# Key cache of a decode step: the second and third pair of heads loaded in one transfer of 64 KB rows

## Chip, cores and metric

The kernel runs on one core of a Trainium2 chip. The metric is the device time of one execution in microseconds (us), lower is better. Several executions were timed, and one was recorded by the hardware profiler; "span" is the time from the first to the last instruction of that execution.

## What is computed

One decode step for one token of width 512: attention over a cache of 16384 keys and values with 8 key/value heads of 128 and 32 query heads (four to a key/value head), then a small block whose sequence mixer sees a sequence of length one, and an MLP.

```python
h  = x + A(layernorm(x))                # A: attention over the cache
h2 = h + B(layernorm(h))                # B: mixer + MLP, weights w1..w4

# A, for the 8 key/value heads:
q = (x @ wq).reshape(1, 1, 32, 128)     # 32 query heads
scores = q @ k^T * 128 ** -0.5          # k_cache [1, 8, 16384, 128], bf16
p = softmax(scores)
o = p @ v                               # v_cache [1, 8, 16384, 128], bf16
A = o.reshape(1, 1, 4096) @ wo

# B: with a sequence of one, every shifted quarter of the mixer is padding (zero),
# so x1 = x, and what is left is
B = x + gelu(layernorm(x) @ w3) @ w4
```

The keys and values together are 67 MB of the 79 MB that are read.

## The kernel before

The heads are worked on in four **pairs** (`PAIRS = 4`). For one pair the keys are 8 MB, laid out over 128 partitions with one row of 64 KB in each (`pair_rows`: 64 partitions for each of the two heads, 256 keys in each partition). The values lie the same way in `vb`. There is one key buffer `kb_all` of 64 KB a partition, cut into two halves `kb[0]` and `kb[1]`, and one value buffer `vb`.

Key loads: pair 0 comes in one load of 8 MB. Pairs 1 to 3 come in two loads of 4 MB (`load_keys(j, y)`), one for each half `y`, and each is issued when the transposes of that half of the pair before have been read out. Value loads: one of 8 MB a pair (`load_values`), issued when the value matmuls of the pair before are done; POOL waits for it with a nop, which releases TensorE. All of these go through SP's queue, in the order of the program: wq, keys 0, values 0, keys 1 (two halves), values 1, and so on; after the keys of pair 3 and the values of pair 3 the weights `wo` (two loads), `w3` and `w4` (four loads), which reuse `kb`.

For one pair the work runs as follows:

1. VectorE transposes the keys (`transpose_keys`, L616) from `kb` into `kt`, half by half; `kt` holds one half. A half has eight pieces; an instruction does one or two of them (`cuts`). A piece was made of two runs of 2 KB, one in each half of the row's half.
2. TensorE computes the scores (`scores`): a clearing matmul (L627) for each half and four matmuls for each of its eight pieces (L633), in a loop with registers, which waits on VectorE's semaphore before every piece.
3. `softmax`: maximum (`mx`, L643), its exchange between partitions over TensorE (L647), exponentials on ScalarE (L655), two transposes into `pt` (L659).
4. Meanwhile TensorE runs a loop of matmuls whose result nobody reads (`P.spin`, fourteen passes of two, L498). Behind that loop, in TensorE's order, come the sum of the softmax (`sums`, L678) and the value matmuls (`values`, L670).
5. `gather` (L687 to L696) brings the result together, and the next pair begins.

TensorE's program for a pair is one loop body that is run four times (`_tensor`). The waits and offsets that change from piece to piece and from pair to pair are held in registers. After the last pair come the product with `wo` (L739), the layer norm, the products with `w3` (L759) and `w4` (L782, L794) and the output.

Of the kernel before, what the change touches and what calls it, by code (L numbers as in the profile page):

```python
# [7 lines left out]
BF16 = mybir.dt.bfloat16  # L8
I32 = mybir.dt.int32
# [340 lines left out]
DH = 128  # L350
# [11 lines left out]
PAIRS = HKV // 2  # L362
RPARTS = 9
QPAD = 4 * 7
KP = 8 * DH
QW = QPAD + 128
SCALE = 1.0 / math.sqrt(DH)
EPS = 1e-5
# [2 lines left out]
def bass_sequential_preLN__gqa_block_cached__mixer_s_mlp__decode_kernel(  # L371
# [13 lines left out]
    with ExitStack() as ctx:  # L385
        sb = lambda name, shape, dt: ctx.enter_context(nc.sbuf_tensor(name, shape, dt))
        ps = lambda name, shape, dt: ctx.enter_context(nc.psum_tensor(name, shape, dt))
        P = Program(nc, ctx)
# [54 lines left out]
        hT = sb("hT", [128, NCH, 32], FP32)  # L443
        hcol = sb("hcol", [128, NHC, 32], BF16)
        fin = sb("fin", [64, 256], BF16)
        kb_all = sb("kb", [128, 256 * DH], BF16)
        kb = [kb_all[:, i * 128 * DH:(i + 1) * 128 * DH] for i in range(2)]
        vb = sb("vb", [128, 256 * DH], BF16)
        kt = sb("kt", [128, 128 * DH], BF16)
# [12 lines left out]
        def load(name, dst, src, key, by="SP", also=()):  # L462
            P.op(by, lambda e: e.dma_start(dst, src), w=[key, *also], dma=name)

        def pair_rows(src, j):
            return src[0, 2 * j:2 * j + 2].rearrange("g (u t) d -> (g u) (t d)", u=64)

        def load_keys(j, y):
            n = 128 * DH
            load(f"k{y}", kb[y][:, :], pair_rows(A_k_cache, j)[:, y * n:(y + 1) * n], ("r", y, 0),  # L470
                 also=[("r", y, i) for i in range(1, RPARTS)])

        def load_values(j):
            load("v", vb[:, :], pair_rows(A_v_cache, j), ("v", 0), also=[("landed", 0)])
# [19 lines left out]
        def copies(col, n):  # L494
# [4 lines left out]
                                      start=True, stop=True)  # L499
# [27 lines left out]
        def variance(i):  # L527
# [7 lines left out]
            for n in range(1 + i):  # L535
# [6 lines left out]

        load("x4", x4[:, :], A_x[0, 0:1, :].rearrange("o (q j) -> (o q) j", q=4), "x4", "ACT")
        load("wq", wq_sb[:, 0:NCH * HQ * DH], A_wq.rearrange("(p k) c -> p (k c)", k=NCH), ("v", 0), also=[("v", x) for x in range(1, VP)])
        load("k", kb_all[:, :], pair_rows(A_k_cache, 0), ("r", 0, 0),
             also=[("r", y, i) for y in range(2) for i in range(RPARTS) if y or i])

        dve(lambda e: e.memset(mean4[:, :], -1.0 / (32 * D)), w=["mean4"])
        dve(lambda e: e.memset(ident_f[:, :], 0.0), w=["ident_f"])
# [8 lines left out]
            r=["ident", "x4"], w=["quarter"])  # L558
        pe(lambda e: e.matmul(O_ps[0][:, 0:128], quarter[:, :, :].rearrange("p q u -> p (q u)"), x4[:, :],
                              start=True, stop=True), r=["quarter"], w=[("O", 0)], bank=[("O", 0)])  # L560
# [7 lines left out]
             r=["ident_f"], w=["swapped"])  # L568

        dve(lambda e: e.tensor_reduce(row32[:, :], ident_f[:, :].rearrange("p (c r) -> p r c", c=4), AX.X, ALU.add),  # L570
            r=["ident_f"], w=["row32"])
        dve(lambda e: e.tensor_reduce(maskdd[:, :], ident_f[:, :].rearrange("p (n d) -> p d n", d=4), AX.X, ALU.add),
            r=["ident_f"], w=["maskdd"])
# [35 lines left out]
                qcol[lo:hi, :, :, 0].rearrange("p n (j h) -> p n j h", h=REP)), r=["qcol"], w=["qb"])  # L609


        def transpose_keys(y, cuts):
            for t, n in zip(cuts, [b - a for a, b in zip(cuts, [*cuts[1:], 8])]):
                view = lambda x, t=t, n=n: x[:, :].bitcast(I32).rearrange("p (x l w) -> p x (l w)", x=2, l=64)[
                    :, :, t * 512:(t + n) * 512]
                P.op("DVE", lambda e, view=view: e.transpose(view(kt), view(kb[y])),  # L616
                     r=[("r", y, i) for i in range(RPARTS)], w=[("kt", t + i) for i in range(n)], worth=n)

        def key_piece(at, n):
            part = kt[:, :].rearrange("p (x f) -> p x f", x=2)[:, :, bass.ds(at, KP)]  # L620
            return part.rearrange("p x (l b s e) -> p b e x l s", l=8, b=2, s=32, e=2)[:, n // 2, n % 2, :, :, :]

        none = qn[:, 0, 0:1]

# [35 lines left out]
                    r=["p"], w=["pt"])  # L660

        def values(j):
            tiles = vb[:, :].rearrange("p (x c l d) -> p x l c d", x=4, c=8, l=8)
            for x in range(VP):
                P.part("value", j, x)
                for it in range(16 // VP):
                    for ct in range(4):
                        l, ch = 2 * it + ct // 2, ct % 2
                        l += 32 // VP * x
                        pe(lambda e, l=l, ct=ct, ch=ch: e.matmul(  # L670
                            O_ps[0][32 * ct:32 * ct + 32, :], pt[:, l, ch, :, :].rearrange("p g u -> p (g u)"),
                            tiles[:, l // 8, l % 8, 4 * ch:4 * ch + 4, :], start=(l < 2), stop=(l >= 30)),
                           r=[("landed", x), "pt"], w=[("O", 0)], bank=[("O", 0)])

        def sums(j):

            P.spin(14)
            pe(lambda e: e.matmul(n_ps[0:32, 32:33], zd[:, :], acc[:, :], start=True, stop=True),  # L678
               r=["acc", "zd", "pt"], w=["n"], bank=["mn"])
            dve(lambda e: e.reciprocal(den[:, :], n_ps[0:32, 32:33]), r=["n"], w=["den"], bank=["mn"])  # L680
# [21 lines left out]
        for j in range(PAIRS):  # L702
            P.part("query", j)
            dve(lambda e, j=j: e.tensor_copy(qn[:, :, :], qb[:, :, j, :]), r=["qb"], w=["qn"])
            for y in range(2):
                P.part("half", j, y)
                transpose_keys(y, (0, 2, 4, 6) if j < PAIRS - 1 else range(8) if y else (0, 1, 2, 4, 6))
                scores(j, y)
                if j < PAIRS - 1:
                    load_keys(j + 1, y)  # L710
            P.part("middle", j)
            softmax(j)
            sums(j)
            values(j)
            P.part("rest", j)
            gather(j)
            if j < PAIRS - 1:
                load_values(j + 1)
# [29 lines left out]
        s = st[1]  # L748
# [87 lines left out]
```

## Time and profile before

| | |
|---|---|
| median of 3 executions | 189.88 us (189.8 to 190.06) |
| the profiled execution | 189.89 us, span 188.4 us |
| VectorE, TensorE matmuls, ScalarE, busy | 115.8, 137.8, 9.3 us |
| DMA | 79.19 MB, 2605 packets, mean 420 GB/s over the span |
| SP's queue, share of the 16 engines | 97.9% |
| keys, values | 2 x 4 MB a pair (pair 0: 8 MB), 8 MB a pair |

How to read the rows that follow: the profile lists instructions by source line (L616 is line 616 of the kernel before), engine and operation. DVE is VectorE, PE the matmuls of TensorE, PEld its weight loads, ACT ScalarE, POOL GpSimd, SPq the instruction stream of SyncE, which issues the loads. A row of a timeline begins with the start in us from the span's start and the length in us; x8 counts merged instructions; the square bracket is the idle time of that engine just before, and what ended it. Rows of the list of DMA issues end with the us from issue to landing. Where no bracket stands, the engine had no idle time to speak of.

### The profile page before, as it was taken

To read this page: it belongs to the slowest core of one execution; us is meant where nothing else is said; L and a number is where in the kernel's file an instruction comes from. 1 tells how busy PE (TensorE), PEld (TensorE's weight loads), DVE (VectorE), ACT (ScalarE), POOL (GpSimd) and SP (SyncE) were. 2 spreads that over 40 slices of the span, in tenths; PEclk is the share of its full clock that TensorE was granted. 3 is DMA by queue.
4 is the path that set the end of the run, shared out by engine and by line. 5 is a ranking of instruction groups with operands and counts; after the bars stand their busy time and mean duration, and the time that the engine had idled before them with its cause. 6 is when DMAs were issued, how large, how long until landed. Compare 5 with 4: busy or idle time off the path is not lost.

```text
span 188.4 us, 2532 instructions
## 1 busy us (share of the span) xinstructions
PE 137.8 (73%) x820; PEld 59.3 (31%) x824; DVE 115.8 (61%) x141; ACT 9.3 (5%) x16; POOL 5.9 (3%) x11
## 2 busy tenths in 40 slices
PE   1009700599989639998990999999319999886874
PEld 1004200234434413443450344345103433432332
DVE  4900741999645299994508999551449897513154
ACT  3000000000020000000200000020000000500011
POOL 1900000000000000000000000000000000000010
PEclk9999985569999975999998599999955999999998
DMA  6999999999799998999999999997999998899994
GB/s 223 445 445 445 445 445 445 445 445 445 334 445 445 445 543 362 417 389 403 445 445 445 445 445 445 445 445 334 445 445 445 556 403 362 362 440 450 397 411 183
DMA packets 2605, 79.19 MB, mean 420 GB/s; under 512 B 298, under 2 KB 300, under 8 KB 812
## 3 DMA queue, kind: packets, MB, share of 16 engines
q1 hardware_dynamic: 2596, 79.17, 97.9%
q8 instruction: 1, 0.02, 0.0%
q10 hardware_dynamic: 8, 0.00, 0.0%
HBM read 79.17 MB, written 0.00 MB: 420 GB/s over the span
## 4 chain that ended last, share of the span: by engine, by line
DMA 45%; PE 36%; DVE 16%; issue 2%; ACT 0%; SPq 0%; DVEq 0%
DMA kb<-in_A_k_cache_dram 32%; PE banks L633 22%; DMA kb<-in_B_w_dram 13%; DVE kt L616 12%; PE banks L498 6%; PE banks L670 4%; DVE mx L643 1%; PE banks L627 1%; DVE od L690 1%; PE banks L647 1%; PE banks L759 1%; PE banks L694 0%; DVE od L687 0%; DVE osum L785 0%; PE banks L782 0%
## 5 line engine op out<-in xcount | busy, mean ns | idle before, releaser
L616 DVE STREAM_TRANSPOSE kt<-kb 128x2048 int32<-128x2048 int32 (+1 forms) x37 | 71.0, 1985 | 10.4 <-DMA kb<-in_A_k_cache_dram 10.4
L633 PE MATMUL banks<-kt,qn 128*128 x256 | 69.1, 426 | 0.1
L633 PEld LDWEIGHTS banks<-kt,qn 128*128 x256 | 26.8, 105 | 41.0 <-issue 21.5
L498 PE MATMUL banks<-xn 128*128 128x512 bf16 x126 | 28.6, 381 | 0.0
L627 PE MATMUL banks<-qn 128*128 128x512 bf16 x8 | 3.9, 490 | 23.9 <-DVE kt L616 23.9
L498 PEld LDWEIGHTS banks<-xn 128*128 128x128 bf16 x130 | 12.7, 99 | 15.8 <-issue 2.4
L593 PE MATMUL banks<-vb,xn 128*128 x32 | 8.5, 432 | 9.7 <-DVE xn L584 9.7
L670 PE MATMUL banks<-vb,pt 128*32 128x512 bf16 x256 | 14.7, 379 | 0.7 <-POOLq L475 0.7
L659 DVE STREAM_TRANSPOSE pt<-p_sb 64x1024 bf16<-64x1024 bf16 x8 | 9.9, 1239 | 5.4 <-ACT p_sb L655 5.3
L655 ACT ACTIVATE p_sb<-banks,bias 128x1024 bf16<-128x1024 f32 x4 | 4.5, 1114 | 155.4 <-DVE nmh L651 155.4
L670 PEld LDWEIGHTS banks<-vb,pt 128*32 128x32 bf16 x256 | 8.7, 97 | 4.7 <-POOLq L475 0.8
L687 DVE TENSOR_SCALAR od<-banks,rowc 128x128 f32<-128x128 f32 x4 | 1.4, 351 | 14.2 <-PE banks L670 14.2
L643 DVE TENSOR_REDUCE mx<-banks 128x1 f32<-128x1024 f32 x4 | 4.9, 1224 | 8.1 <-PE banks L633 8.1
L627 PEld LDWEIGHTS banks<-qn 128*128 128x128 bf16 x8 | 0.8, 100 | 25.8 <-issue 25.4
L600 DVE STREAM_TRANSPOSE qcol<-banks 64x1024 f32<-64x1024 f32 x4 | 4.8, 1226 | 6.6 <-PE banks L593 6.6
L593 PEld LDWEIGHTS banks<-vb,xn 128*128 128x128 bf16 x32 | 3.5, 108 | 14.3 <-issue 11.6
L539 POOL TENSOR_TENSOR st<-st,expo 128x1 f32<-128x1 f32 (+1 forms) x2 | 1.3, 630 | 175.4 <-DVE st L537 175.4
L506 PE MATMUL banks<-mean 128*128 128x512 f32 (+1 forms) x12 | 6.5, 622 | 0.0
L694 PE MATMUL banks<-od,zo 128*32 128x128 f32 x8 | 1.6, 285 | 6.5 <-DVE od L690 6.5
L680 DVE RECIPROCAL den<-banks 32x1 f32<-32x1 f32 x4 | 0.6, 155 | 7.8 <-PE banks L678 7.8
L690 DVE SCALAR_TENSOR_TENSOR od<-banks,rowc,od 128x128 f32<-128x128 f32 x12 | 4.2, 351 | 0.4
L647 PE MATMUL banks<-mxd,mean 128*128 128x128 f32 x8 | 2.0, 326 | 2.4 <-DVE mxd L644 2.4
(81 smaller groups left out, 49.5 us busy)
## 6 DMA issues: line engine op xcount, KB each, us to landing
kb<-in_A_k_cache_dram SPq DMA_DIRECT2D x6, 4096.0 KB, 24.9
vb<-in_A_wq_dram SPq DMA_DIRECT2D x1, 4096.0 KB, 12.3
kb<-in_A_wo_dram SPq DMA_DIRECT2D x1, 3584.0 KB, 28.5
kb<-in_B_w_dram SPq DMA_DIRECT2D x1, 1792.0 KB, 24.2
kb<-in_B_w_dram SPq DMA_DIRECT2D x1, 896.0 KB, 26.0
kb<-in_B_w_dram SPq DMA_DIRECT2D x1, 640.0 KB, 27.1
kb<-in_A_wo_dram SPq DMA_DIRECT2D x1, 512.0 KB, 29.4
kb<-in_B_w_dram SPq DMA_DIRECT2D x1, 256.0 KB, 27.2
```

What stands on the lines that cost most here:

```text
L498: P.unread = lambda e: e.matmul(banks[:, 7, :], copies(xn[:, 0:1], 128), copies(xn[:, 0:1], 512), start=True, stop=True)
L506: pe(lambda e: e.matmul(banks[:, 7, 0:n], mean4[:, :], copies(mean4[:, 0:1], n), start=True, stop=True), r=["mean4"], w=["spare1"])
L593: pe(lambda e, k=k: e.matmul(row[:, bass.ds(P.b, 512)], copies(xn[:, k:k + 1], 128), wq_k[:, k, bass.ds(P.c, REP * DH)], start=(k == 0), s ...
L600: dve(lambda e, g=g, b=b, half=half: e.transpose(qcol[64 * g:64 * g + 64, 2 * b:2 * b + 2, :, :].rearrange("p e m u -> p (e m u)"), half.r ...
L616: P.op("DVE", lambda e, view=view: e.transpose(view(kt), view(kb[y])), r=[("r", y, i) for i in range(RPARTS)], w=[("kt", t + i) for i in r ...
L627: pe(lambda e: e.matmul(row[:, bass.ds(P.y, 512)], copies(none, 128), copies(none, 512), start=True, stop=False, skip_group_check=True), r ...
L633: pe(lambda e, n=n: e.matmul(row[:, bass.ds(P.y, 512)], qn[:, n, bass.ds(P.q, 128)], key_piece(P.k, n), start=False, stop=(n == 3), skip_g ...
L643: dve(lambda e: e.tensor_reduce(mx[:, :], s_all, AX.X, ALU.max), r=[("s", 0), ("s", 1)], w=["mx"], **both)
L655: act(lambda e: e.activation(p_sb[:, :], s_all, ACTF.Exp, bias=bias[:, 0:1], scale=float(SCALE), accum_out=acc[:, :]), r=[("s", 0), ("s", ...
L659: dve(lambda e, g=g: e.transpose(pt[64 * g:64 * g + 64, :, :, g, :], p_sb[64 * g:64 * g + 64, :]), r=["p"], w=["pt"])
L670: pe(lambda e, l=l, ct=ct, ch=ch: e.matmul(O_ps[0][32 * ct:32 * ct + 32, :], pt[:, l, ch, :, :].rearrange("p g u -> p (g u)"), tiles[:, l ...
L690: dve(lambda e, block=block, c=c: e.scalar_tensor_tensor(od[:, :], block, rowc[:, c:c + 1], od[:, :], ALU.mult, ALU.add), r=[key, "rowc", ...
```

## The change

The keys of pairs 1 and 2 come in one load of 8 MB (64 KB a row), as those of pair 0 do; pair 3 keeps its two halves. To let such a load begin before the pair ahead has been read to the end, the key buffer grows by 8 KB a partition and each pair's keys lie 4 KB lower than those of the pair before (`BASE`): pair 0 at 8 KB, pair 1 at 4 KB, pairs 2 and 3 at 0. The last sixteenth of pair 0 and of pair 1 thus lies above what the next load writes; the instruction that reads it has a key of its own (`tail`), and the load waits for the other fifteen sixteenths alone. For this the last two pieces of the second half are transposed one by one.

A piece is now one contiguous sixteenth of the row (4 KB) in place of two runs of 2 KB, with the views of `key_piece` and `values` to match; `KP`, the step of a piece, doubles. The loop of unread matmuls runs eleven passes in place of fourteen in every pair. The first half of pair 3 is transposed in four instructions of two pieces, where it was two of one and three of two.

```diff
--- before.py
+++ after.py
@@ -362,7 +362,8 @@
 PAIRS = HKV // 2
 RPARTS = 9
 QPAD = 4 * 7
-KP = 8 * DH
+KP = 16 * DH
+BASE = (2 * KP, KP, 0, 0)
 QW = QPAD + 128
 SCALE = 1.0 / math.sqrt(DH)
 EPS = 1e-5
@@ -443,7 +444,7 @@
         hT = sb("hT", [128, NCH, 32], FP32)
         hcol = sb("hcol", [128, NHC, 32], BF16)
         fin = sb("fin", [64, 256], BF16)
-        kb_all = sb("kb", [128, 256 * DH], BF16)
+        kb_all = sb("kb", [128, BASE[0] + 256 * DH], BF16)
         kb = [kb_all[:, i * 128 * DH:(i + 1) * 128 * DH] for i in range(2)]
         vb = sb("vb", [128, 256 * DH], BF16)
         kt = sb("kt", [128, 128 * DH], BF16)
@@ -465,10 +466,14 @@
         def pair_rows(src, j):
             return src[0, 2 * j:2 * j + 2].rearrange("g (u t) d -> (g u) (t d)", u=64)
 
-        def load_keys(j, y):
+        def load_keys(j, y=None):
             n = 128 * DH
-            load(f"k{y}", kb[y][:, :], pair_rows(A_k_cache, j)[:, y * n:(y + 1) * n], ("r", y, 0),
-                 also=[("r", y, i) for i in range(1, RPARTS)])
+            if y is None:
+                load("k", kb_all[:, BASE[j]:BASE[j] + 2 * n], pair_rows(A_k_cache, j), ("r", 0, 0),
+                     also=[("r", y, i) for y in range(2) for i in range(RPARTS) if y or i] + [("tail", j)])
+            else:
+                load(f"k{y}", kb[y][:, :], pair_rows(A_k_cache, j)[:, y * n:(y + 1) * n], ("r", y, 0),
+                     also=[("r", y, i) for i in range(1, RPARTS)])
 
         def load_values(j):
             load("v", vb[:, :], pair_rows(A_v_cache, j), ("v", 0), also=[("landed", 0)])
@@ -542,8 +547,7 @@
 
         load("x4", x4[:, :], A_x[0, 0:1, :].rearrange("o (q j) -> (o q) j", q=4), "x4", "ACT")
         load("wq", wq_sb[:, 0:NCH * HQ * DH], A_wq.rearrange("(p k) c -> p (k c)", k=NCH), ("v", 0), also=[("v", x) for x in range(1, VP)])
-        load("k", kb_all[:, :], pair_rows(A_k_cache, 0), ("r", 0, 0),
-             also=[("r", y, i) for y in range(2) for i in range(RPARTS) if y or i])
+        load_keys(0)
 
         dve(lambda e: e.memset(mean4[:, :], -1.0 / (32 * D)), w=["mean4"])
         dve(lambda e: e.memset(ident_f[:, :], 0.0), w=["ident_f"])
@@ -609,16 +613,18 @@
                 qcol[lo:hi, :, :, 0].rearrange("p n (j h) -> p n j h", h=REP)), r=["qcol"], w=["qb"])
 
 
-        def transpose_keys(y, cuts):
+        def transpose_keys(j, y, cuts):
             for t, n in zip(cuts, [b - a for a, b in zip(cuts, [*cuts[1:], 8])]):
-                view = lambda x, t=t, n=n: x[:, :].bitcast(I32).rearrange("p (x l w) -> p x (l w)", x=2, l=64)[
-                    :, :, t * 512:(t + n) * 512]
-                P.op("DVE", lambda e, view=view: e.transpose(view(kt), view(kb[y])),
-                     r=[("r", y, i) for i in range(RPARTS)], w=[("kt", t + i) for i in range(n)], worth=n)
+                at = BASE[j] + (8 * y + t) * KP
+                apart = BASE[j] and y and t == 7
+                P.op("DVE", lambda e, t=t, n=n, at=at: e.transpose(
+                    kt[:, t * KP:(t + n) * KP].bitcast(I32), kb_all[:, at:at + n * KP].bitcast(I32)),
+                     r=[("tail", j)] if apart else [("r", y, i) for i in range(RPARTS)],
+                     w=[("kt", t + i) for i in range(n)], worth=n)
 
         def key_piece(at, n):
-            part = kt[:, :].rearrange("p (x f) -> p x f", x=2)[:, :, bass.ds(at, KP)]
-            return part.rearrange("p x (l b s e) -> p b e x l s", l=8, b=2, s=32, e=2)[:, n // 2, n % 2, :, :, :]
+            part = kt[:, bass.ds(at, KP)]
+            return part.rearrange("p (l b s e) -> p b e l s", l=16, b=2, s=32, e=2)[:, n // 2, n % 2, :, :]
 
         none = qn[:, 0, 0:1]
 
@@ -660,7 +666,7 @@
                     r=["p"], w=["pt"])
 
         def values(j):
-            tiles = vb[:, :].rearrange("p (x c l d) -> p x l c d", x=4, c=8, l=8)
+            tiles = vb[:, :].rearrange("p (y c x l d) -> p y x l c d", y=2, c=8, x=2, l=8)
             for x in range(VP):
                 P.part("value", j, x)
                 for it in range(16 // VP):
@@ -669,12 +675,12 @@
                         l += 32 // VP * x
                         pe(lambda e, l=l, ct=ct, ch=ch: e.matmul(
                             O_ps[0][32 * ct:32 * ct + 32, :], pt[:, l, ch, :, :].rearrange("p g u -> p (g u)"),
-                            tiles[:, l // 8, l % 8, 4 * ch:4 * ch + 4, :], start=(l < 2), stop=(l >= 30)),
+                            tiles[:, l // 16, l // 8 % 2, l % 8, 4 * ch:4 * ch + 4, :], start=(l < 2), stop=(l >= 30)),
                            r=[("landed", x), "pt"], w=[("O", 0)], bank=[("O", 0)])
 
         def sums(j):
 
-            P.spin(14)
+            P.spin(11)
             pe(lambda e: e.matmul(n_ps[0:32, 32:33], zd[:, :], acc[:, :], start=True, stop=True),
                r=["acc", "zd", "pt"], w=["n"], bank=["mn"])
             dve(lambda e: e.reciprocal(den[:, :], n_ps[0:32, 32:33]), r=["n"], w=["den"], bank=["mn"])
@@ -704,10 +710,12 @@
             dve(lambda e, j=j: e.tensor_copy(qn[:, :, :], qb[:, :, j, :]), r=["qb"], w=["qn"])
             for y in range(2):
                 P.part("half", j, y)
-                transpose_keys(y, (0, 2, 4, 6) if j < PAIRS - 1 else range(8) if y else (0, 1, 2, 4, 6))
+                transpose_keys(j, y, range(8) if y and j == PAIRS - 1 else (0, 2, 4, 6, 7) if y else (0, 2, 4, 6))
                 scores(j, y)
-                if j < PAIRS - 1:
+                if j == PAIRS - 2:
                     load_keys(j + 1, y)
+                elif j < PAIRS - 2 and y:
+                    load_keys(j + 1)
             P.part("middle", j)
             softmax(j)
             sums(j)
```

## The prediction

> **What bounds the kernel now.** I read the page first: the share of the DMA engines and the chain of waits.
>
> ```profile
> span 188.4 us, 2532 instructions
> q1 hardware_dynamic: 2596, 79.17, 97.9%
> DMA 45%; PE 36%; DVE 16%; issue 2%; ACT 0%; SPq 0%; DVEq 0%
> ```
>
> The one load queue is busy for 97.9% of the span, and the chain changes hands between transfers and computing. So I laid the queue's own timetable (the timeline of SP: start and length of each issue) beside the landings (the list of DMA issues, asked for around one issue at a time; the last number is us from issue to landing).
>
> ```profile
> 0.74 0.40 SPq L463 DMA_DIRECT2D vb<-in_A_wq_dram  x1
> 1.19 0.42 SPq L463 DMA_DIRECT2D kb<-in_A_k_cache_dram  x1
> 22.43 0.33 SPq L463 DMA_DIRECT2D vb<-in_A_v_cache_dram  x1
> 50.16 0.33 SPq L463 DMA_DIRECT2D kb<-in_A_k_cache_dram  x1
> 64.38 0.33 SPq L463 DMA_DIRECT2D vb<-in_A_v_cache_dram  x1
> 133.21 0.33 SPq L463 DMA_DIRECT2D vb<-in_A_v_cache_dram  x1
> ```
> ```profile
> vb<-in_A_wq_dram SPq DMA_DIRECT2D x1, 4096.0 KB, 12.3
> kb<-in_A_k_cache_dram SPq DMA_DIRECT2D x1, 31.2
> vb<-in_A_v_cache_dram SPq DMA_DIRECT2D x1, 29.3
> kb<-in_A_k_cache_dram SPq DMA_DIRECT2D x1, 4096.0 KB, 21.0
> vb<-in_A_v_cache_dram SPq DMA_DIRECT2D x1, 26.1
> vb<-in_A_v_cache_dram SPq DMA_DIRECT2D x1, 34.9
> ```
>
> Issue plus time to landing: wq at 13.0, first keys at 32.4, first values at 51.7, the second half of pair 1's keys at 71.2, pair 1's values at 90.5, pair 3's values at 168.1. Steps: an 8 MB load takes 19.3 us, two 4 MB loads 71.2 - 51.7 = 19.5, the next 8 MB 19.3. The queue runs without a hole, and a pair costs it 38.8 us.
>
> Then the VectorE timeline, where each pair's work begins and ends.
>
> ```profile
> 32.47 17.66 DVE L616 STREAM_TRANSPOSE kt<-kb 128x2048 int32<-128x2048 int32 x8 [6.46 <-DMA kb<-in_A_k_cache_dram]
> 52.43 1.22 DVE L643 TENSOR_REDUCE mx<-banks 128x1 f32<-128x1024 f32 x1 [2.29 <-PE banks L633]
> 66.84 17.64 DVE L616 STREAM_TRANSPOSE kt<-kb 128x2048 int32<-128x2048 int32 x8
> 86.77 1.23 DVE L643 TENSOR_REDUCE mx<-banks 128x1 f32<-128x1024 f32 x1 [2.29 <-PE banks L633]
> 101.30 17.66 DVE L616 STREAM_TRANSPOSE kt<-kb 128x2048 int32<-128x2048 int32 x8
> 121.25 1.22 DVE L643 TENSOR_REDUCE mx<-banks 128x1 f32<-128x1024 f32 x1 [2.29 <-PE banks L633]
> 139.04 8.95 DVE L616 STREAM_TRANSPOSE kt<-kb 128x1024 int32<-128x1024 int32 x5 [3.17 <-DMA kb<-in_A_k_cache_dram]
> 148.74 9.13 DVE L616 STREAM_TRANSPOSE kt<-kb 128x1024 int32<-128x1024 int32 x8 [0.75 <-DMA kb<-in_A_k_cache_dram]
> 159.12 1.22 DVE L643 TENSOR_REDUCE mx<-banks 128x1 f32<-128x1024 f32 x1 [1.25 <-PE banks L633]
> ```
>
> Pairs 1 and 2 have no idle time before their first transpose: keys were there, and VectorE and TensorE set the pace, 34.4 us a pair (101.30 - 66.84). That is 4.4 us a pair less than the queue needs, so computing, late after the start, has caught up with the queue at pair 3: it waits 3.17 us for the first half of the keys. From there transfers lead, but by little.
>
> ```profile
> 60.58 0.40 PE L670 MATMUL banks<-vb,pt 128*32 128x512 bf16 x3
> 161.04 6.29 PE L498 MATMUL banks<-xn 128*128 128x512 bf16 x28
> 163.08 2.49 DVE L659 STREAM_TRANSPOSE pt<-p_sb 64x1024 bf16<-64x1024 bf16 x2 [1.33 <-ACT p_sb L655]
> 168.16 0.40 PE L670 MATMUL banks<-vb,pt 128*32 128x512 bf16 x4 [0.67 <-POOLq L475]
> 176.71 1.91 PE L739 MATMUL banks<-kb,o_b 128*32 128x512 bf16 x32 [0.17 <-DMA kb<-in_A_wo_dram]
> 182.29 0.94 PE L759 MATMUL banks<-kb,hc 128*32 128x448 bf16 x16 [0.34 <-DMA kb<-in_B_w_dram]
> 186.60 0.12 PEld L794 LDWEIGHTS banks<-kb,hcol 128*32 128x32 bf16 x8 [0.20 <-DMA kb<-in_B_w_dram]
> ```
>
> The value matmuls of pair 3, and each of the three weight products behind them, wait for their load by 0.67, 0.17, 0.34 and 0.20 us (POOL's nop stands for the values' landing). That is all the cover a later computing chain has.
>
> **The change part by part.**
>
> *One load in place of two, for pairs 1 and 2.* The queue gains the difference of 19.5 and 19.3 or 19.4, about 0.1 us a pair by landings rounded to 0.1; bounds 0 and 0.2 each. I take 0.1 twice.
>
> The Trainium skill (DMA: Bandwidth & Descriptors, "Anatomy of one DMA") fits a load's time, for the path of GpSimd, as 2.0 us plus its bytes over 436 GB/s. If those 2 us occupied the queue, two loads fewer would give 4 us; the steps above show some 0.1, because the next load streams meanwhile.
>
> *The issue moves from the half to fifteen sixteenths.* Before, pair 1's first half was issued when half of pair 0 was transposed. Now SP waits for seven instructions of two pieces and one of one piece: 17.66 less one piece, 9.13 / 8 = 1.14, so 16.5, with one more start 16.6, and the issue stands at 32.47 + 16.6 = 49.1. The queue drains at 51.7. What an issue needs before its bytes flow is seen at the start: wq lands 12.3 us after its issue, of which 4 MB are 19.3 / 2 = 9.7, so 2.6. 49.1 + 2.6 = 51.7: exactly in time. Below, no gain is possible, since bytes cannot flow before the queue is empty; above, the wq figure is from an empty queue and the same lead recurs at pair 2, so I allow 0 to 0.6 us a load and take 0. Pair 1's keys then land at 71.1, its values at 90.4, pair 2's keys at 109.8. Behind SP's longer wait stand only later loads. The value load of pair 1 goes out at 64.38 less what the loop saves, 63.1, and is needed by 71.1 - 2.6 = 68.5. With the steps below and the 3.8 us from value matmuls to issue (64.38 - 60.58), those of pairs 2 and 3 go out 30.6 us after a pair's first transpose, at 101.8 and 140.5, and are needed by 107.2 and 145.9: 5 us of cover each.
>
> *No transpose before 8 MB have landed.* This is the cost. Pair 2 began at 101.30; now it begins at 109.9. From first transpose to `mx` the three full pairs take 19.96, 19.93 and 19.95 us, so `mx` stands at 129.85.
>
> *The last two pieces of a pair in two instructions.* They come one by one, so one might take the 2.29 us before `mx` for 1.25, as pair 3 has it. The weight loads of pair 1's last three pieces speak against that:
>
> ```profile
> 83.57 0.66 PEld L633 LDWEIGHTS banks<-kt,qn 128*128 x4 [0.22 <-issue]
> 84.64 0.56 PEld L633 LDWEIGHTS banks<-kt,qn 128*128 x4 [0.41 <-issue]
> 85.69 0.56 PEld L633 LDWEIGHTS banks<-kt,qn 128*128 x4 [0.49 <-issue]
> ```
>
> They follow each other every 1.05 us with idle time put to "issue": TensorE's sequencer needs that long for a turn of its loop, whichever piece lies ready. Bounds: 0 and 1.04 us; I take 0.
>
> *Eleven passes in place of fourteen.* 28 matmuls take 6.29 us, so six fewer take 6 x 0.22 = 1.3 off. This counts whole: `pt` is ready at 163.08 + 2.49 = 165.57, before even the shortened loop ends at 161.04 + 6.29 - 1.3 = 166.0.
>
> *Contiguous pieces, other strides for scores and values.* The same elements in the same number of matmuls; I take 0, bounds minus and plus 0.1 us a pair (the four transposing stretches above differ by 0.02).
>
> *The sum.* From `mx` to the next pair's first transpose: 66.84 - 52.43 = 14.4 and 101.30 - 86.77 = 14.5; less 1.3 it is 13.2. Pair 3 begins at 129.85 + 13.2 = 143.05 in place of 139.04; both halves of its keys are there by then or before they are needed (138.9 and 148.5, against 143.05 and 151.9). Its `mx` stands at 143.05 + 19.95 = 163.0 in place of 159.12. From `mx` to the value matmuls pair 0, which had its values, took 60.58 - 52.43 = 8.15; less 1.3 it is 6.85, so 169.85 in place of 168.16: 1.7 us later, and now behind its load (167.9), not waiting for it. The later waits fall away one after another: 1.7 - 0.17 - 0.34 - 0.20 = 1.0. The profiled execution took 189.89 us with a span of 188.4; 1.0 on it gives **190.9**. Its time is that of the median (189.88), so no correction between the two.
>
> One cost has a range of its own: TensorE's clock at the beginning of a pair.
>
> ```profile
> 34.92 0.61 PE L627 MATMUL banks<-qn 128*128 128x512 bf16 x1 [12.60 <-DVE kt L616]
> 39.00:41.00 2.00, 2.00 (x7) 0.59 0.68 295
> 41.00:43.00 2.00, 2.00 (x11) 1.00 1.21 524
> ```
>
> The windows' column after the count is the granted clock: half until about 40.6 (0.59 of that stretch), so 5.7 us after the first matmul. Pairs 2 and 3 will start at other moments and may find other such stretches.
>
> The Trainium skill (TensorE: Matmul & The Clock Gate, Part 1) says that activity is judged in free-running windows of 3.4 us, so that a cold stretch lies between one and two windows, up to 6.8 us. By that rule a bad phase is 1.1 us colder than here, half of which is lost work: up to 0.5 us a pair, and the sum would be 191.9; none of it in a good phase, since the sequencer and the transposes hold the pace then. Trace and rule agree as far as 5.7 lies between; I take 0 and keep it for the range.
>
> **The rivals.**
>
> *The last piece alone shortens the score tail.* If the loop turn hides nothing, pair 2 gives back 1.04 us; pair 3 has its eight single pieces already. Then 1.7 becomes 0.7, which the same waits swallow, and what is left is the queue's 0.2: 189.7. For it: pair 3's 1.25. Against it: the three weight-load rows.
>
> *The issue comes too late.* Each miss opens a hole in the queue that moves everything after it, computing included. With 0.6 us at both loads 190.9 + 1.2 = 192.1. For it: the lead of 2.6 is no longer than the start-up of 2.6. Against it: the engines need not be idle when the new load's descriptors arrive, and part of the 2.6 is landing, not starting.
>
> *Faster: long rows stream better than the landings show.* If the merged load saved more than 0.5 us each time, pair 2's keys would land over 1.0 us earlier, everything behind would move along, and the loss above be gone; at 1.0 us each the time is 190.9 - 1.8 = 189.1. The steps of 19.3 to 19.5 us leave hardly room for it: the 64 KB rows are in the trace already, as first keys and values.
>
> **How the numbers follow.** My forecast 0.70 (its own range 190.5 to 191.9, with the clock's phase and the strides); short tail 0.13, no change; late issue 0.14, slower; better streaming 0.03, faster. What a measurement of this kernel can tell from no change is about 0.2%, 0.4 us. The range of eight in ten leaves out the fast side, most of the short tail and the worst of the late issues: 190.0 to 192.4. Faster 0.03, same 0.13, slower 0.84.
>
> **What would show it.** Right: SP's second key issue near 49.1 with no hole at 51.7; pair 2's first transpose near 109.9, pair 3's near 143 without an idle time for DMA; value matmuls of pair 3 near 169.9 with no wait for POOL; the waits before the three weight products gone. Wrong: 1.3 instead of 2.3 us before `mx` in pairs 0 to 2 (short tail); key loads landing later than 71.1 and 109.8 (late issue) or clearly earlier (streaming). If pair 3 still idles for its keys, my chain through pair 2 is too long.

## The result, and the profile after

| | before | changed |
|---|---|---|
| median of 6 executions | 189.75 us (189.62 to 190.06) | 190.67 us (190.45 to 190.97) |
| the profiled execution | 189.89 us, span 188.4 us | 190.69 us, span 189.4 us |

The changed kernel is slower: ratio 1.0048, 95% interval 1.0037 to 1.0058. The forecast was 190.9. (Lines have moved: L616 is now L620, L627 L633, L633 L639, L643 L649, L670 L676, L739 L747, L759 L767, L794 L802.)

The page first.

```profile
span 189.4 us, 2456 instructions
q1 hardware_dynamic: 2308, 79.17, 97.3%
DMA 40%; PE 37%; DVE 19%; issue 3%; ACT 0%; SPq 0%; DVEq 0%
```

The same bytes in 288 packets fewer; in the chain that ended last, 5% of the span has gone from DMA, three of the five to VectorE. SP's timeline and the landings (us from issue to landing, asked for around each issue) say where.

```profile
22.96 0.33 SPq L464 DMA_DIRECT2D vb<-in_A_v_cache_dram  x1
49.26 0.33 SPq L464 DMA_DIRECT2D kb<-in_A_k_cache_dram  x1
63.17 0.33 SPq L464 DMA_DIRECT2D vb<-in_A_v_cache_dram  x1
87.97 0.33 SPq L464 DMA_DIRECT2D kb<-in_A_k_cache_dram  x1
101.87 0.33 SPq L464 DMA_DIRECT2D vb<-in_A_v_cache_dram  x1
140.57 0.33 SPq L464 DMA_DIRECT2D vb<-in_A_v_cache_dram  x1
```
```profile
vb<-in_A_v_cache_dram SPq DMA_DIRECT2D x1, 28.9
kb<-in_A_k_cache_dram SPq DMA_DIRECT2D x1, 21.9
vb<-in_A_v_cache_dram SPq DMA_DIRECT2D x1, 27.4
kb<-in_A_k_cache_dram SPq DMA_DIRECT2D x1, 21.9
vb<-in_A_v_cache_dram SPq DMA_DIRECT2D x1, 27.5
```

The first values, issued at 22.96, land at 51.9; pair 1's keys at 71.2, its values at 90.6, pair 2's keys at 109.9, pair 3's values at 168.1. Each 8 MB still takes 19.3 us, so the queue has no hole (no time without bytes) in this execution. The lead, the time from a key load's issue until the load ahead of it has landed, was only 2.6 us both times (51.9 - 49.26, 90.6 - 87.97). The whole stream ends where it did; what has moved is the computing:

```profile
71.30 17.72 DVE L620 STREAM_TRANSPOSE kt<-kb 128x2048 int32<-128x2048 int32 x9 [5.61 <-DMA kb<-in_A_k_cache_dram]
91.23 1.22 DVE L649 TENSOR_REDUCE mx<-banks 128x1 f32<-128x1024 f32 x1 [2.21 <-PE banks L639]
110.00 17.72 DVE L620 STREAM_TRANSPOSE kt<-kb 128x2048 int32<-128x2048 int32 x9 [5.47 <-DMA kb<-in_A_k_cache_dram]
129.93 1.23 DVE L649 TENSOR_REDUCE mx<-banks 128x1 f32<-128x1024 f32 x1 [2.21 <-PE banks L639]
143.14 17.90 DVE L620 STREAM_TRANSPOSE kt<-kb 128x2048 int32<-128x2048 int32 x12
163.07 1.23 DVE L649 TENSOR_REDUCE mx<-banks 128x1 f32<-128x1024 f32 x1 [2.03 <-PE banks L639]
```

VectorE, which never waited for the keys of pairs 1 and 2, now waits 5.61 and 5.47 us for their 8 MB. Pair 3, which waited 3.17 us for its keys, no longer waits at all (no bracket) and begins 4.1 us later than before. TensorE, from there to the end:

```profile
165.00 4.97 PE L503 MATMUL banks<-xn 128*128 128x512 bf16 x22
169.91 0.40 PE L676 MATMUL banks<-vb,pt 128*32 128x512 bf16 x3
178.29 1.91 PE L747 MATMUL banks<-kb,o_b 128*32 128x512 bf16 x32
183.46 0.94 PE L767 MATMUL banks<-kb,hc 128*32 128x448 bf16 x16
187.26 0.57 PE L802 MATMUL banks<-kb,hcol 128*32 128x128 bf16 x28
```

The brackets that named a load at the value matmuls and at the three weight products are gone. The lateness shrinks along these rows: 169.91 - 168.16 = 1.75 us at the value matmuls, 1.58 at L747, 1.17 at L767. The end of the span is 1.0 later.

### The profile page after: what moved, and what is told of

The parts are those of the page before. It is cut to its first block, busy times and chain, and to the rows that moved or that the text cites. A ratio compares the mean times of both kernels' runs of the same rounds, so it can differ in the third digit from the quotient of the medians.

```text
span 189.4 us, 2456 instructions
## 1 busy us (share of the span) xinstructions
PE 131.4 (69%) x796; PEld 57.0 (30%) x800; DVE 115.9 (61%) x143; ACT 9.3 (5%) x16; POOL 5.9 (3%) x11
## 4 chain that ended last, share of the span: by engine, by line
DMA 40%; PE 37%; DVE 19%; issue 3%; ACT 0%; SPq 0%; DVEq 0%
DMA kb<-in_A_k_cache_dram 40%; PE banks L639 22%; DVE kt L620 14%; PE banks L503 7%; PE banks L676 4%; DVE mx L649 1%; PE banks L633 1%; DVE od L696 1%; PE banks L747 1%; PE banks L653 1%; PE banks L511 1%; PE banks L767 0%; PE banks L700 0%; DVE od L693 0%; DVE osum L793 0%
## 5 line engine op out<-in xcount | busy, mean ns | idle before, releaser
L620 DVE STREAM_TRANSPOSE kt<-kb 128x2048 int32<-128x2048 int32 (+1 forms) x39 | 71.1, 1891 | 17.1 <-DMA kb<-in_A_k_cache_dram 17.1
L639 PE MATMUL banks<-kt,qn 128*128 x256 | 67.7, 416 | 0.0
L639 PEld LDWEIGHTS banks<-kt,qn 128*128 x256 | 26.4, 103 | 40.0 <-issue 20.8
L633 PE MATMUL banks<-qn 128*128 128x512 bf16 x8 | 3.9, 492 | 32.6 <-DVE kt L620 32.6
L503 PE MATMUL banks<-xn 128*128 128x512 bf16 x102 | 23.3, 381 | 0.0
L676 PE MATMUL banks<-vb,pt 128*32 128x512 bf16 x256 | 14.8, 379 | 0.0
L503 PEld LDWEIGHTS banks<-xn 128*128 128x128 bf16 x106 | 10.3, 99 | 12.9 <-issue 2.4
L633 PEld LDWEIGHTS banks<-qn 128*128 128x128 bf16 x8 | 0.8, 100 | 34.7 <-issue 34.4
L676 PEld LDWEIGHTS banks<-vb,pt 128*32 128x32 bf16 x256 | 9.5, 97 | 3.3
L649 DVE TENSOR_REDUCE mx<-banks 128x1 f32<-128x1024 f32 x4 | 4.9, 1224 | 8.7 <-PE banks L639 8.7
L585 DVE COPY zo<-rowgh 128x32 f32<-128x32 f32 x1 | 3.6, 3628 | 0.0
L585 DVE COPY zd<-maskgh 128x32 f32<-128x32 f32 x1 | 3.6, 3557 | 0.0
## 6 DMA issues: line engine op xcount, KB each, us to landing
kb<-in_A_k_cache_dram SPq DMA_DIRECT2D x2, 4096.0 KB, 20.5
```

Source lines behind the costliest of these rows:

```text
L503: P.unread = lambda e: e.matmul(banks[:, 7, :], copies(xn[:, 0:1], 128), copies(xn[:, 0:1], 512), start=True, stop=True)
L585: dve(lambda e, z=z, m=m: e.tensor_copy(z[:, :].rearrange("p (n d) -> p n d", d=4), m[:, :, :].rearrange("p g h -> p (g h)").unsqueeze(2). ...
L620: P.op("DVE", lambda e, t=t, n=n, at=at: e.transpose(kt[:, t * KP:(t + n) * KP].bitcast(I32), kb_all[:, at:at + n * KP].bitcast(I32)), r=[ ...
L633: pe(lambda e: e.matmul(row[:, bass.ds(P.y, 512)], copies(none, 128), copies(none, 512), start=True, stop=False, skip_group_check=True), r ...
L639: pe(lambda e, n=n: e.matmul(row[:, bass.ds(P.y, 512)], qn[:, n, bass.ds(P.q, 128)], key_piece(P.k, n), start=False, stop=(n == 3), skip_g ...
L649: dve(lambda e: e.tensor_reduce(mx[:, :], s_all, AX.X, ALU.max), r=[("s", 0), ("s", 1)], w=["mx"], **both)
```

## The experiments

All were run beside the kernel before, in three series, each on one chip: p1_only, p2_only, spin14 and before_spin11 (the kernel before: 189.81); shift2_spin14, no_shift, spin9 and p1_lead (189.86); after_again, shift2, shift2_spin9 and p1_shift4 (189.91). The record doesn't name the chip of the first result above.

**Which pair costs: p1_only and p2_only.** The edits to the changed kernel:

```diff
# p1_only                                   # p2_only
-BASE = (2 * KP, KP, 0, 0)
+BASE = (KP, 0, 0, 0)                       # BASE = (KP, KP, 0, 0)
-if j == PAIRS - 2:
-    load_keys(j + 1, y)
-elif j < PAIRS - 2 and y:
-    load_keys(j + 1)
+if 1 <= j <= PAIRS - 2:                    # if j in (0, PAIRS - 2):
+    load_keys(j + 1, y)
+elif j == 0 and y:                         # elif j < PAIRS - 2 and y:
+    load_keys(j + 1)
```

In p2_only the halves of pair 1 are also placed at `BASE[j]`, and the key of its own (`apart`) holds for pair 1 alone.

> Only pair 1's keys come in one load; pair 2's come in two halves again (buffers shifted once, by 4 KB). Theory (cover): the loss is made at pair 2, whose transposes start only when 8 MB have landed and whose lateness reaches the end through pair 3; pair 1's late start is absorbed. So pair 2 starts at 71.3 + 33.1 = 104.4 as soon as pair 1 is done, pair 3 waits for its first half again (first transpose near 139.0), the value matmuls of pair 3 wait for their load, and the time is that of before, 189.7. Rival (queue): each merged load costs the queue the same; then half of the loss remains, 190.2. Rival (loop or strides): the loss is in what all pairs share, the time stays at 190.7.

> Only pair 2's keys come in one load; pair 1's come in two halves. Theory (cover): pair 1 starts early again, near 65.7, but pair 2 cannot start before its 8 MB have landed, 110.0, and everything behind it stands as in the changed kernel: 190.7. Rival (queue): one merged load less, half of the loss, 190.2. Rival (both late starts add): 189.7 to 190.2.

Measured: p1_only 190.15 (189.64 to 190.93, 12 executions), ratio 1.0025, interval 1.0011 to 1.0039; p2_only 190.81 (190.67 to 190.92), ratio 1.0051, interval 1.0038 to 1.0064. VectorE's rows of p1_only, and the value matmuls of its pair 3:

```profile
104.19 17.72 DVE L620 STREAM_TRANSPOSE kt<-kb 128x2048 int32<-128x2048 int32 x9
139.00 8.89 DVE L620 STREAM_TRANSPOSE kt<-kb 128x2048 int32<-128x2048 int32 x4 [1.58 <-DMA kb<-in_A_k_cache_dram]
168.05 3.64 PE L676 MATMUL banks<-vb,pt 128*32 128x512 bf16 x64 [1.99 <-POOLq L480]
```

and VectorE's of p2_only (its lines stand one lower, L620 is L621):

```profile
65.58 17.70 DVE L621 STREAM_TRANSPOSE kt<-kb 128x2048 int32<-128x2048 int32 x9
110.01 17.72 DVE L621 STREAM_TRANSPOSE kt<-kb 128x2048 int32<-128x2048 int32 x9 [11.21 <-DMA kb<-in_A_k_cache_dram]
143.16 17.89 DVE L621 STREAM_TRANSPOSE kt<-kb 128x2048 int32<-128x2048 int32 x12
```

p2_only is the clear one: pair 1 begins 5.7 us earlier than in the changed kernel and gains nothing; its finished VectorE idles 11.21 us, pair 2 begins at 110.01, and the time is that of the changed kernel. One merged load, at pair 2, makes the whole loss: pair 2 starts 8.7 us later than in the kernel before (110.0, 101.30), more than the shorter loop and pair 3's wait of 3.17 us can take up. In the profiled execution of p1_only (189.87) the waits for loads are back and the loss is gone, as expected. But its executions spread over 1.3 us, which was not expected; p1_lead and p1_shift4 below bear on that.

**The passes: spin14, spin9 and before_spin11.**

```diff
-P.spin(11)
+P.spin(14)     # spin14; spin9: P.spin(9); before_spin11: 14 -> 11 in the kernel before
```

> The changed kernel with fourteen passes again. Theory (cover): pairs 2 and 3 are no longer hidden by loads, so six matmuls of 0.22 us count whole twice, 2 x 1.3: 193.3; pair 3 starts at 144.5, its value matmuls near 172.5. Rival (the loop lies beside other work, as in the kernel before): 190.7. If only pair 3 counted: 192.0.

> The kernel before with eleven passes. Theory (cover): computing waits for loads at pair 3 anyway, so nothing changes: 189.75, with the wait of the value matmuls of pair 3 grown from 0.67 to about 2.0 us. Rival (each pass counts wherever it stands): 1.3 or 2.6 us less, 188.4 or 187.1.

> The changed kernel with nine passes. Theory (computing sets the end): the loop then ends before the transposed probabilities are ready (6.45 us after mx begins; the value matmuls come 6.84 after it now), so only some 0.35 us a pair can be had, twice: 190.0. Rival (whole passes count): 4 x 0.22 twice, 188.9; rival (loads set the end): 190.7.

Measured: spin14 in two groups, three executions from 193.09 to 193.19 and three from 194.91 to 195.58 (median 194.05, ratio 1.0224, interval 1.0179 to 1.027). spin9 in two groups as well, four from 189.84 to 190.17 and eight from 191.59 to 192.55 (median 191.81, ratio 1.0072, interval 1.0041 to 1.0103). before_spin11 190.44 (189.68 to 190.67), ratio 1.0024, interval 1.0009 to 1.0039.

The lower groups are the forecasts for computing that nothing hides: 193.14 - 190.67 = 2.5 for three passes more (2.6 expected; the 190.67 is from another series), 190.0 for two passes fewer. That nine passes bring less than whole passes is in spin9's TensorE row: what comes behind its loop waits for `pt`.

```profile
166.69 4.10 PE L503 MATMUL banks<-xn 128*128 128x512 bf16 x18
171.27 0.22 PE L684 MATMUL banks<-acc,zd 128*32 128x1 f32 x2 [0.48 <-DVE pt L665]
```

The upper groups are dealt with below. before_spin11 is a miss of another kind: not the same but slower. TensorE's row of the value matmuls in pair 3 and the windows around it (us, busy, count, granted clock, DMA), then the same two windows of the kernel before:

```profile
168.02 5.27 PE L670 MATMUL banks<-vb,pt 128*32 128x512 bf16 x64 [1.98 <-POOLq L475]
168.00:170.00 2.00, 1.98 (x20) 0.50 1.03 444
170.00:172.00 2.00, 2.00 (x28) 0.66 1.07 459
```
```profile
168.00:170.00 2.00, 1.84 (x36) 1.00 1.08 459
170.00:172.00 2.00, 1.79 (x36) 1.00 1.06 459
```

The wait grew to 1.98 us as expected, but TensorE has nothing to do in it, the clock is granted at half when the values land, and the 64 matmuls take 5.27 us in place of 3.64. The weight products behind no longer wait for their loads, so of these 1.6 us the span keeps 0.7 (189.1 against 188.4). In this execution, then, the fourteen passes of the kernel before were not idle padding: with them the clock was still up when the load came. That the same happened in the other executions of before_spin11 is not shown, since only this one was profiled.

The Trainium skill (TensorE: Matmul & The Clock Gate, Part 1) has the clock fall after an idle window of 3.4 us that runs free of the program. Here a wait of 1.98 us sufficed once and, in p1_only's profiled execution, did not (1.99 us, 3.64). That one and the same wait did both fits a window that runs free; that 2 us without matmuls were enough does not fit a whole idle one, and the measurement decides. By the two windows above the clock then stood at half from 168.0 to 171.4, for 3.4 us.

**The issue that comes too late: no_shift.**

```diff
-BASE = (2 * KP, KP, 0, 0)
+BASE = (0, 0, 0, 0)
```

> The changed kernel without the shift of the buffers: each merged load waits for all sixteen sixteenths and goes out 1.1 us later. Theory (the lead is just long enough): both loads leave a hole of about 1.1 us and the time is 190.7 + 2 x 1.1 = 192.9, up to 195 where a part of the load starts late as well. Rival (there is slack in the queue): 190.7 to 191.2.

Measured: 193.88 (193.74 to 194.35), ratio 1.0217, interval 1.0194 to 1.0239: 1.0 beyond the 192.9 of two holes of 1.1, inside the wider case. SP's rows and the landings of its two merged loads:

```profile
50.15 0.33 SPq L464 DMA_DIRECT2D kb<-in_A_k_cache_dram  x1
89.99 0.33 SPq L464 DMA_DIRECT2D kb<-in_A_k_cache_dram  x1
kb<-in_A_k_cache_dram SPq DMA_DIRECT2D x1, 21.9
kb<-in_A_k_cache_dram SPq DMA_DIRECT2D x1, 23.0
```

They land at 72.1 and 113.0, 0.9 and 3.1 us later than in the changed kernel. So the queue has no slack to speak of. The second load needed 1.1 us more than the first for the same bytes and the same lead (1.5 and 1.4 us), which the theory of the lead alone does not say.

**The upper groups: shift2_spin14, then after_again, shift2 and shift2_spin9.** In spin14's profiled execution (194.91) pair 2 begins at

```profile
111.59 4.50 DVE L620 STREAM_TRANSPOSE kt<-kb 128x2048 int32<-128x2048 int32 x2 [5.82 <-DMA kb<-in_A_k_cache_dram]
```

1.6 us after the changed kernel's 110.00, though its load had gone out no later (at 87.89). That points to the queue, not to the passes. A shift of 8 KB a pair lets a load go out one piece, some 1.1 us, earlier (shift2_spin14 has fourteen passes besides):

```diff
-BASE = (2 * KP, KP, 0, 0)
+BASE = (4 * KP, 2 * KP, 0, 0)
-apart = BASE[j] and y and t == 7
+apart = BASE[j] and y and t >= 6
```

> The changed kernel with fourteen passes and buffers shifted by 8 KB a pair, so that each merged load waits for fourteen sixteenths and goes out 1.1 us earlier. Theory (late issue, for the spread of the fourteen-pass kernel: its profiled execution has one group of bytes of pair 2's keys landing 1.6 us behind the rest, its first bytes flowing 3.25 us after the issue): with the longer lead no execution is late, all lie near 193.1 to 193.3. Rival (the spread has another cause): about half of the executions stay near 195.

Measured: 193.89 (193.71 to 194.31), ratio 1.0209, interval 1.0191 to 1.0228. The 195s are gone, but none of the executions reaches 193.1: half a hit. Since the chips differed, the changed kernel itself was run again, beside this shift with eleven and with nine passes.

> The changed kernel once more, beside the three that follow. Theory (cover): 190.7, as measured. What is open is how often a merged load begins late in it: in the nine-pass kernel eight executions of twelve lay near 192 and four near 190.0, and in the profiled one parts of pair 2's load began up to 3.7 us after the issue. If the lead of 2.6 us alone decides this, some executions of the changed kernel lie 1 to 2 us above 190.7; if the changed kernel is not touched, all lie within 0.3.

> The changed kernel with buffers shifted by 8 KB a pair: both merged loads go out 1.1 us earlier, eleven passes. Theory (late issue): never slower than the changed kernel beside it, and with a narrower spread; 190.7 where no load is late, since an issue before the queue is empty moves no byte. Rival (an earlier issue helps by itself): under 190.4. Rival (the start-up of a load, not the lead, sets the spread): 191 to 192, as in the fourteen-pass kernel with this shift, which lay 0.6 to 1.1 us above 193.1.

> As the one before, with nine passes. Theory (cover): the value matmuls follow the transposed probabilities directly, 0.35 us a pair less than with eleven passes, twice: 190.0 where no load is late. Late issue: fewer executions near 192 than the eight of twelve without the longer shift. Rival (the passes keep the clock up): slower than eleven passes, with value matmuls of 5 us in place of 3.6.

Measured on one chip: after_again 192.05 (one execution at 190.66, five from 191.75 to 192.6), ratio 1.0103, interval 1.0075 to 1.013; shift2 191.36 (191.0 to 191.67), ratio 1.0076, interval 1.0063 to 1.0089; shift2_spin9 190.8 (190.46 to 191.11), ratio 1.0042, interval 1.003 to 1.0054. So the changed kernel has the upper group too. Pair 2's key load in after_again's profiled execution (192.13), and where pair 2 begins:

```profile
88.24 0.33 SPq L464 DMA_DIRECT2D kb<-in_A_k_cache_dram  x1
kb<-in_A_k_cache_dram SPq DMA_DIRECT2D x1, 23.1
111.43 2.31 DVE L620 STREAM_TRANSPOSE kt<-kb 128x2048 int32<-128x2048 int32 x1 [6.62 <-DMA kb<-in_A_k_cache_dram]
```

The same issue, 23.1 us to landing in place of 21.9. The list of DMA, asked for 89 to 93 us only, shows when packets began: 40 slices of 0.1 us, a digit where some did. First the changed kernel's first profiled execution, then after_again.

```profile
DMA  0000009999990000000000000000009999999000
```
```profile
DMA  0000000090900999099900900000000099900009
```

In the first all parts of the load begin within 0.6 us, from 89.6 to 90.2, as the value load ahead of them ends. In the second they begin from 89.8 to 91.3; the last at 3.0 us from the issue. The Trainium skill (DMA: Bandwidth & Descriptors, "Latency and other measured facts") gives some 0.6 us to the first byte on this path. The program's first load, `wq` into an empty queue, shows more in the kernel before: packets began 1.0 to 2.1 us after its issue; and for the last of the 16 engines 3.0 us were needed here. What is lost so is not made up: pair 2 begins 111.43 - 110.00 = 1.4 us later, pair 3's values land at 169.5 in place of 168.1, and the profiled times differ by 192.13 - 190.69 = 1.4.

shift2 cuts this but does not end it. Its pair 1 load, with a lead of 3.7 us, still was late:

```profile
48.01 0.33 SPq L464 DMA_DIRECT2D kb<-in_A_k_cache_dram  x1
kb<-in_A_k_cache_dram SPq DMA_DIRECT2D x1, 23.9
```

71.9 in place of 71.2, and 20.2 us behind the values ahead of it. Its pair 2 load, with the same lead, was not late (19.3 us behind). The lead alone does not decide, then: in the four profiled executions where pair 1's load went out near 48.0 (shift2, shift2_spin14, shift2_spin9, p1_lead) it landed 20.0 to 20.2 us behind the values, in the five where it went out near 49.1 (the changed kernel, after_again, spin14, spin9, p1_only) 19.3 to 19.7. The earlier issue landed later, and no run here says why. shift2_spin9 lies 0.56 under shift2, near the 0.7 expected of two passes fewer.

**Can pair 1's load be had for nothing: p1_lead and p1_shift4.** p1_only with a larger shift and more passes.

```diff
-BASE = (KP, 0, 0, 0)
+BASE = (2 * KP, 0, 0, 0)        # p1_shift4: (4 * KP, 0, 0, 0)
-apart = BASE[j] and y and t == 7
+apart = BASE[j] and y and t >= 6  # p1_shift4: t >= 4
-P.spin(11)
+P.spin(14)                      # p1_shift4: 13
```

> Only pair 1's keys in one load, buffer shifted by 8 KB, fourteen passes. Theory: the late issue and the clock that falls while pair 3's value matmuls wait for their load (half speed for part of them in the profiled execution of the kernel before with eleven passes) are both gone; pair 1's late start is absorbed; 189.75, the time of before or 0.05 under it, with no execution above 190.1. Rival (a merged load costs by itself): 190.2. Rival (a merged load gains by itself): 189.5 or less.

> Only pair 1's keys in one load, buffer shifted by 16 KB, thirteen passes; the load waits for twelve sixteenths and has a lead of nearly 6 us. Theory: no late load; pair 1's late start is absorbed, since two pairs of 34.0 us from 71.2 end at 139.2, when pair 3's first half lands (139.0); value matmuls wait about 1 us for their load: 189.8, the time of before. Rival (a merged load costs by itself): 190.2 or more. If the clock falls while the value matmuls wait: single executions up to 191.

Measured: p1_lead 190.56 (189.92 to 190.86), ratio 1.0031, interval 1.0019 to 1.0042, a miss; p1_shift4 189.77 (189.56 to 190.13), ratio 0.9997, interval 0.9988 to 1.0006, no difference. Pair 3's first transpose in p1_lead:

```profile
140.75 17.90 DVE L620 STREAM_TRANSPOSE kt<-kb 128x2048 int32<-128x2048 int32 x12
```

I had not multiplied out my own theory: with fourteen passes two pairs take 2 x 34.5 us, and from 71.83 (the load was 0.5 us late there too) they end at 140.8, not at 139: computing is again behind the keys (no bracket). p1_shift4's load, with a lead of 5.9 us, and its pair 3:

```profile
45.70 0.33 SPq L464 DMA_DIRECT2D kb<-in_A_k_cache_dram  x1
kb<-in_A_k_cache_dram SPq DMA_DIRECT2D x1, 25.3
139.08 8.88 DVE L620 STREAM_TRANSPOSE kt<-kb 128x2048 int32<-128x2048 int32 x4
167.96 3.64 PE L676 MATMUL banks<-vb,pt 128*32 128x512 bf16 x64 [1.02 <-POOLq L480]
```

The load lands at 71.0, 19.4 us after the values ahead of it, and 11 executions lie within 0.6 us. This merged load, with a longer lead and with waits behind it that take up its late start, costs nothing and gains nothing that can be measured. No version run here beat the kernel before: its queue had no hole to fill.

## Why the prediction was right, and the step that was too small

Point by point. *The sum* held row by row: key issue 49.1 (49.26), landings 71.1 and 109.8 (71.2, 109.9), pair 2 at 109.9 (110.00), its `mx` at 129.85 (129.93), pair 3 at 143.05 (143.14), `mx` 163.0 (163.07), value matmuls 169.85 (169.91), end plus 1.0 (plus 1.0, the profiled times plus 0.8). p2_only shows the cause, and spin14 and spin9, in their lower groups, that each microsecond at pairs 2 and 3 counted whole.

*The short tail* is refuted: with the last piece alone the idle time before `mx` is 2.21 us, from 2.29, not 1.25. The 1.25 of pair 3, which spoke for it, did not come from single pieces either: pair 3 still has them, and shows 2.03 now that it no longer waits for keys; in p1_only, where it waits for its second half, it is 1.25 again. *Better streaming* is refuted, too: 19.3 us an 8 MB load, as before. *The clock's phase* cost nothing here:

```profile
38.00:40.00 2.00, 2.00 (x10) 0.96 1.21 524
116.00:118.00 2.00, 2.00 (x10) 0.83 1.21 524
142.00:144.00 2.00, 0.41 (x2) 1.00 0.83 360
144.00:146.00 2.00, 0.41 (x2) 0.50 1.21 524
150.00:152.00 2.00, 2.00 (x9) 0.80 1.21 524
```

By these windows the clock came up at 116.7 and 150.8, 4.2 and 5.2 us after the first matmuls of pairs 2 and 3; `mx` came 19.93 us after the first transpose both times, and at pair 0 as well (52.52 - 32.59). Both values lie between the one and two windows of 3.4 us that the prediction took from the Trainium skill (TensorE: Matmul & The Clock Gate, Part 1). Pair 0 does not: there the clock came up at 38.2, 3.1 us after the first matmul at 35.03, so a window need not be busy from its first moment. That the windows run free is plain in this trace: the clock changes at 38.2, 116.7, 144.0 and 150.8 us, and the steps between these, 78.5, 27.3 and 6.8 us, are 23, 8 and 2 times 3.41.

*The late issue* is the term that was mis-sized. I took 0 for it, read from one start-up of 2.6 us with an empty queue, and gave 0.6 us a load as the upper end. The first six executions agreed with 0, and that was luck: in the third series five of six executions of the same kernel were 1.1 to 1.9 us above 190.7. Their median, 192.05, still lies in the range that I gave, but it is the rival's price (192.1 at 0.14), not the forecast's. The rival deserved more: "exactly in time" in a sum of rounded numbers is a coin toss, and a start-up seen once is no bound. Its price was right in size, but the two loads do not share it evenly: in after_again they landed 19.7 and 20.5 us behind the values ahead of them, 0.4 and 1.2 late; in no_shift it was 0.9 at the first and 2.2 more at the second. A longer lead was not safe by itself (3.7 us: 0.9 late at pair 1 in shift2, not late at pair 2). Not late by more than 0.1 were the profiled loads with 5.9 us (p1_shift4) and 8.3 us (p2_only), one of each.

*The eleven passes* were costed at 1.3 us off, twice, which they are. What I did not cost is the other thing they can do: while a load is awaited they hold the clock, as the profiled execution of before_spin11 shows by their absence. In the changed kernel the value matmuls of pair 3 no longer wait, so there it cost nothing.

What stays open: why the last parts of the same load begin 1.1 us later in one execution of the changed kernel than in another (91.3, 90.2), and whether the chip or the moment decides; why pair 1's load landed later when it went out earlier; and how much of p1_only's spread is late loading and how much the clock, since p1_shift4 changed both. A lead of 5 us or more for both merged loads was not tried.

## What to carry to other kernels

When a transfer queue and a chain of computing are nearly level, lay both timetables side by side and add up the waits for loads that computing still has ahead of it. A stage that starts later is free as long as these waits take up the delay (pair 1 in p1_only, 4.2 us late), and what goes beyond them counts whole (pair 2, 8.7 us late). Merging two loads doubles the grain at which the next stage can begin, and where the queue already runs without a hole there is little to win by it. And a refill that goes out just in time by a start-up seen once is not safely in time: the same lead of 2.6 us lost nothing in six executions and over 1 us in five of six others.

## What the hardware did that I had not expected

The 16 DMA engines do not always begin a load together when it is issued shortly before the queue is empty: they began within 0.6 us in the changed kernel's first run and within 1.5 us in after_again, and the delay was still there at the last values (169.5, 168.1). An earlier issue did not always help: pair 1's load landed later when issued near 48.0 than near 49.1. And the filler matmuls in front of a wait were worth 1.6 us at the value matmuls in one profiled execution: without them the clock stood at 0.50 to 0.66 there, 5.27 us in place of 3.64.
